# Second product by seven quarter products, with new load order, in a fused attention and feed-forward kernel

## The chip, the cores and the metric

One core of a Trainium2 chip. The metric is the device time of one execution in microseconds (us). Several executions of each kernel were timed, alternating with the kernel before on the same chip; the median is quoted. All runs in this document were in the normal (fast) state. TensorE's granted clock varies within an execution.

## The reference, cut to what matters

```python
# q, k, v: 8 batches x 8 heads x 576 positions x 64;  w_in: 512x2048;  w_out: 2048x512
k_p = k.reshape(B, H, 72, 8, D).mean(axis=3)          # keys and values pooled by 8
v_p = v.reshape(B, H, 72, 8, D).mean(axis=3)
attn = softmax(q @ k_p^T / sqrt(D))
x = (attn @ v_p) -> 4608 tokens x 512
h = x @ w_in;  g = h * sigmoid(h);  out = g @ w_out   # float32, 4608 x 512
```

## The kernel before

The 4608 tokens are worked off in nine tiles of 512. Each tile has a first product ("up", 64 matmuls of 512 columns, and a Silu on ScalarE) and a second product ("down", 64 matmuls of 512 columns). Tile *t* also carries the attention of batch *t* + 1: small pieces are put between the matmuls at numbered steps ("fillers"). The order written here is the order in which each engine's work stands in its timeline. A "tree" below is the pooling of one batch's k or v on VectorE.

```python
def load_one(b, name, eng=None):          # all of k or v of a batch: 72 x 4096 fp32
    ...
    raw = raw_tile(name, SP, POOL)
    (eng or nc.sync).dma_start(out=raw, in_=src)

def tree(dst, raw):                       # pooling by 8: three adds on VectorE
    w = POOL * D // 2
    while w > D:
        nc.vector.tensor_add(out=raw[:, :, :w], in0=raw[:, :, :w], in1=raw[:, :, w : 2 * w])
        w //= 2
    nc.vector.tensor_add(out=dst, in0=raw[:, :, :D], in1=raw[:, :, D : 2 * D])
...
def down(t, h_T, fillers, ms, last=False):
    ...
            for g in range(KG):                      # 16 blocks of the hidden size
                for m, ps in zip(mm, o_ps):          # token blocks of 128
                    ...
                    nc.tensor.matmul(ps[:, cs], lhsT=h_T[g][:, m * 128 : (m + 1) * 128],
                                     rhs=w_out_sb[:, g, cs], start=(g == 0), stop=(g == KG - 1))
            ... copy to o_sb on VectorE, four stores per token block on SyncE ...
...
for t in range(NT):
    a = t + 1                                        # the batch whose attention runs beside
    ...
    f_up.append((at["k"], lambda: pool_k(a)))        # step 0 of the first product (t > 0)
    f_to.append((50 if t else 13, lambda: pool_v(a)))
    f_to.append((0, lambda: load_q(a + 1)))          # GpSimd's queue
    f_to.append((1, lambda: load_one(a + 1, "k", eng)))              # SyncE's queue
    f_to.append((51 if t else 14, lambda: load_one(a + 1, "v", eng)))
```

The softmax here doesn't subtract the row's maximum and nothing guards it: scores larger than these inputs give would overflow.

## Time and profile before

| | |
|---|---|
| median | 325.02 us (324.83 to 325.92) |
| profiled span, mean granted clock | 323.8 us, 0.989 |
| first tile with all of the start | 0 to 65.73 us |
| second to seventh tile | 33.08 us each |
| eighth tile (no attention beside) | 27.62 us |
| last tile with the tail | 31.97 us |

Three more rows of the busy time by stretches, for the first, the eighth and the last tile, are compared with the changed kernel later (columns: stretch, length, then busy us and count of TensorE, weight loads, VectorE, ScalarE, GpSimd; then granted clock, DMA share, GB/s):

```profile
0.00:65.73 65.73, 57.09 (x477) 34.21 (x478) 32.19 (x53) 33.20 (x70) 15.83 (x28) 0.95 0.98 229
264.21:291.83 27.62, 27.62 (x129) 12.51 (x128) 2.77 (x4) 11.21 (x18) 0.00 (x0) 1.00 0.16 41
291.83:323.80 31.97, 27.83 (x145) 13.90 (x142) 3.62 (x6) 9.92 (x17) 0.00 (x0) 1.00 0.16 42
```

In the eighth tile TensorE's busy time is the whole length; in the last, 4 us of the length are not TensorE's.

### The profile page before, as it was taken

The numbers are of one execution on the slowest core, as the hardware profiler recorded it, in microseconds if no ns is written. First come the engines' busy times: TensorE is split into PE (matmuls) and PEld (weight loads), VectorE is DVE, ScalarE is ACT, GpSimd is POOL, SyncE is SP. The second block draws the span as 40 slices with busy tenths as digits, with TensorE's granted clock in tenths as the row PEclk, the third lists the DMA queues.
The fourth block names the chain that finished last, engine by engine and source line by source line (L and its number), as shares of the span: only waits on it lengthen the run. The fifth ranks groups of instructions, "written<-read, shape, count | busy, mean of one in ns | idle before, by whom it ended". The sixth has DMA issues, their size and how long they took to land.

```text
span 323.8 us, 5075 instructions
## 1 busy us (share of the span) xinstructions
PE 311.0 (96%) x2032; PEld 157.0 (48%) x2032; DVE 141.6 (44%) x219; ACT 176.5 (55%) x308; POOL 18.7 (6%) x32
## 2 busy tenths in 40 slices
PE   7899958999999999999999999999999999999994
PEld 3767533444444544454445444544454444444443
DVE  5444761386237633763375337542755230010011
ACT  1478723466656665666565656565656567405500
POOL 5930000000000000000000000000000000000000
PEclk9999995999999999999999999999999999999999
DMA  7999998728722772278327832635200220031023
GB/s 275 257 210 258 238 209 199 200 70 179 180 61 64 171 187 68 66 161 183 88 68 151 178 102 65 145 87 129 65 0 2 65 60 8 7 86 39 0 51 83
DMA packets 23280, 38.15 MB, mean 118 GB/s; under 512 B 3032, under 2 KB 7384, under 8 KB 23256
## 3 DMA queue, kind: packets, MB, share of 16 engines
q1 hardware_dynamic: 16008, 27.73, 32.8%
q0 software_dynamic: 6192, 8.32, 15.4%
q10 hardware_dynamic: 1056, 1.77, 1.5%
q8 instruction: 16, 0.26, 0.4%
q14 instruction: 8, 0.07, 0.1%
HBM read 36.70 MB, written 9.44 MB: 142 GB/s over the span
## 4 chain that ended last, share of the span: by engine, by line
PE 82%; DMA 15%; POOL 1%; issue 1%; SPq 0%; DVE 0%; ACTq 0%; ACT 0%; POOLq 0%
PE o_ps L317 37%; PE hp_ps L286 34%; DMA w_out_sb<-in_moe_w_out_dram 10%; PE sc_ps L199 4%; DMA w_in_sb<-in_moe_w_in_dram 3%; PE nu_ps L243 2%; PE den_ps L221 2%; DMA q_st<-in_q_dram 2%; PE qT_ps L128 2%; POOL w_in_sb L385 1%; SPq L301 0%; DMA out_dram<-o_sb 0%; ACTq L358 0%; PE kT_ps L173 0%; POOL w_out_sb L396 0%
## 5 line engine op out<-in xcount | busy, mean ns | idle before, releaser
L317 PE MATMUL o_ps<-w_out_sb,h_T 128*128 128x512 bf16 (+1 forms) x592 | 143.6, 378 | 4.4 <-DMA w_out_sb<-in_moe_w_out_dram 3.9
L286 PE MATMUL hp_ps<-xT,w_in_sb 128*128 128x512 bf16 (+2 forms) x620 | 131.1, 364 | 0.6 <-ACT h_T L292 0.6
L292 ACT ACTIVATE h_T<-hp_ps 128x512 bf16<-128x512 f32 (+2 forms) x155 | 87.6, 567 | 58.4 <-PE hp_ps L286 57.6
L286 PEld LDWEIGHTS <-w_in_sb 128*128 128x128 bf16 x620 | 59.0, 98 | 57.7 <-issue 1.3
L317 PEld LDWEIGHTS <-h_T 128*128 128x128 bf16 x592 | 55.9, 99 | 60.7 <-issue 11.5
L212 ACT ACTIVATE es<-sc_ps 72x576 bf16<-72x576 f32 x57 | 36.9, 647 | 47.4 <-PE sc_ps L199 47.3
L329 DVE COPY o_sb<-o_ps 128x512 f32<-128x512 f32 (+1 forms) x36 | 24.5, 682 | 83.0 <-PE o_ps L317 82.2
L153 DVE TENSOR_TENSOR raw<-raw 72x2048 f32<-72x2048 f32 (+1 forms) x28 | 49.0, 1750 | 5.0 <-DMA raw<-in_k_dram 4.5
L251 DVE TENSOR_TENSOR xT<-nu_ps,rec 128x288 bf16<-128x288 f32 x64 | 26.2, 453 | 52.1 <-ACT rec L231 33.8
L199 PE MATMUL sc_ps<-qT,kz 128*72 128x288 bf16 x114 | 24.0, 294 | 0.8 <-DVE qT L134 0.7
L134 DVE COPY qT<-qT_ps 128x640 bf16<-128x640 bf16 (+1 forms) x32 | 14.6, 458 | 20.2 <-PE qT_ps L128 20.0
L199 PEld LDWEIGHTS <-kz 128*72 128x72 bf16 x128 | 14.6, 116 | 15.2 <-issue 3.2
L230 ACT ACTIVATE lnd<-den_ps 128x288 f32<-128x288 f32 x30 | 12.1, 402 | 10.1 <-PE den_ps L221 10.1
L128 PEld LDWEIGHTS <-q_bf 128*128 128x128 bf16 x144 | 10.5, 98 | 8.6 <-issue 2.0
L260 ACT ACT_TABLE_LOAD x8 | 10.3, 1283 | 6.7 <-DMA k_st<-in_k_dram 6.6
L243 PE MATMUL nu_ps<-es,vp 72*32 72x288 bf16 x256 | 13.5, 287 | 0.4 <-DVE xT L251 0.4
L231 ACT ACTIVATE rec<-lnd 128x288 f32<-128x288 f32 x30 | 13.3, 442 | 0.9
L117 POOL DMA_DIRECT2D q_bf<-in_q_dram x7 | 5.0, 713 | 151.1 <-PE qT_ps L128 150.3
L128 PE MATMUL qT_ps<-ident,q_bf 128*128 128x128 bf16 x144 | 13.1, 219 | 0.6 <-ACT kz L431 0.6
L263 ACT ACT_TABLE_LOAD x9 | 11.5, 1283 | 0.2
L180 DVE COPY kz<-kT_ps 64x288 bf16<-64x288 bf16 x28 | 8.5, 305 | 4.7 <-PE kT_ps L173 4.3
L221 PE MATMUL den_ps<-es,ones 72*32 72x288 bf16 x128 | 10.2, 296 | 0.0
(41 smaller groups left out, 82.8 us busy)
## 6 DMA issues: line engine op xcount, KB each, us to landing
out_dram<-o_sb SPq DMA_DIRECT2D x140, 64.0 KB
raw<-in_k_dram SPq DMA_DIRECT2D x7, 1152.0 KB
raw<-in_v_dram SPq DMA_DIRECT2D x7, 1152.0 KB
q_bf<-in_q_dram POOLq DMA_DIRECT2D x7, 576.0 KB, 6.1
w_in_sb<-in_moe_w_in_dram POOLq DMA_DIRECT2D x8, 256.0 KB, 8.4
w_out_sb<-in_moe_w_out_dram POOLq DMA_DIRECT2D x4, 512.0 KB, 26.1
q_st<-in_q_dram SPq DMA_DIRECT2D x2, 320.0 KB
v_st<-in_v_dram SPq DMA_DIRECT2D x2, 288.0 KB
```

The costliest lines, as they stand in the source:

```text
L128: nc.tensor.transpose(qT_ps[:, j, :], st["q_bf"][:, a, 2 * D * (j0 + j) : 2 * D * (j0 + j + 1)], ident,)
L134: (copy or nc.vector.tensor_copy)(dst[:, a, j0 : j0 + n], qT_ps.rearrange("d j (s p) -> d j s p", p=QP))
L153: nc.vector.tensor_add(out=raw[:, :, :w], in0=raw[:, :, :w], in1=raw[:, :, w : 2 * w])
L199: nc.tensor.matmul(sc[u][:, :HS], lhsT=kz[b % 2][:, f, 2 * pr + u, :], rhs=st["qT"][:, 2 * pr + u, :], start=True, stop=True,)
L212: nc.scalar.activation(es, sc_ps[:, :, :HS], func=AF.Exp, scale=score_scale)
L221: nc.tensor.matmul(den_ps[32 * hh : 32 * (hh + 1), :HS], lhsT=ones, rhs=es[hh // 2][:, hh % 2, :], start=True, stop=True,)
L243: nc.tensor.matmul(nu_ps[32 * hh : 32 * (hh + 1), :HS], lhsT=st["vp"][:, 4 * g + hh, c::2], rhs=es[hh // 2][:, hh % 2, :], start=True, sto ...
L251: nc.vector.tensor_mul(out=xT[:, 2 * g + c, cols], in0=nu[c][:, :HS], in1=rec)
L286: nc.tensor.matmul(hp_ps[:, :n], lhsT=w_in_sb[:, kk, g * 128 : (g + 1) * 128], rhs=xT[:, kk, t * NTT + n0 : t * NTT + n0 + n], start=(kk = ...
L292: nc.scalar.activation(h_T[g][:, n0 : n0 + n], hp_ps[:, :n], func=AF.Silu)
L317: nc.tensor.matmul(ps[:, cs], lhsT=h_T[g][:, m * 128 : (m + 1) * 128], rhs=w_out_sb[:, g, cs], start=(g == 0), stop=(g == KG - 1),)
L329: nc.vector.tensor_copy(out=o_sb[:, cs], in_=ps[:, cs])
```

## The change

Its intent is to take an eighth of the second product's work from TensorE. In tiles 1 to 8 the 2 x 2 x 2 quarter products become Strassen's seven, for which sums of halves of the hidden tile (VectorE, every tile) and of the second weight (GpSimd, once) are needed. To make room on VectorE, the first of the three pooling adds is done by the load: SyncE loads the first half of every pooled group and GpSimd's queue adds the other half onto it while loading. Batch 1's loads come in pieces by heads, batch 2's later, behind the first stores, so that they do not share the DMA engines with the second weight. ("Half" and "rest" below are these two parts of one load; "hidden sums" and "weight sums" are the sums that the seven products need.) Batch 0's attention is reordered to give ScalarE its exps back to back. The last tile's stores are split over two queues.

```diff
+    def load_rest(b, name):
+        nc.gpsimd.dma_start(out=batches[b][f"{name}_raw"],
+                            in_=source(b, name)[:, :, PH:], accum_op=ALU.add)
+    def hidden_sum(n, k0, k1):                 # five sums, 128 x 2048 bf16 each, in pieces
+        nc.vector.tensor_tensor(out=h_sum[n][:, ks, :], in0=quarter(*a, ks), in1=quarter(*b, ks), op=op)
+    def weight_sum(n, i):                      # five sums in four pieces of 128 x 512 bf16
+        nc.gpsimd.tensor_tensor(out=out, in0=in0, in1=in1, op=op)
+    def down_quarters(t, fillers, last=False):
+        ...                                    # 7 x 16 matmuls of 256 columns in three banks
 ... in the loop over the tiles:
+        if t == 0:                             # three sums into w_sum, second product of tile 0
+            for i in range(PW):
+                for n in range(2, 5):
+                    f_down.append((30 + 8 * i, lambda n=n, i=i: weight_sum(n, i)))
+        if t == 1:                             # two sums in place, first product of tile 1
+            for n in range(2):
+                for i in range(PW):
+                    f_up.append((12, lambda n=n, i=i: weight_sum(n, i)))
-            f_to.append((50 if t else 13, lambda: pool_v(a)))
+            f_to.append((10 if t else 13, lambda: pool_v(a)))
-                f_to.append((1, lambda: load_one(a + 1, "k", eng)))
-                f_to.append((51 if t else 14, lambda: load_one(a + 1, "v", eng)))
+                f_to.append((1 if t else 34, lambda: load_one(a + 1, "k")))
+                f_to.append((2 if t else 44, lambda: load_rest(a + 1, "k")))
+                f_to.append((11 if t else 36, lambda: load_one(a + 1, "v")))
+                f_to.append((12 if t else 54, lambda: load_rest(a + 1, "v")))
 ... cut: the new places of scores and values, batch 0's order, batch 1's loads by heads, the last stores
```

## The prediction

> **What bounds the kernel now.** I read the page's busy table first, then the chain of waits, then the busy time by stretches, and last the timeline of the stretches in which the chain is not TensorE.
>
> ```profile
> PE 311.0 (96%) x2032; PEld 157.0 (48%) x2032; DVE 141.6 (44%) x219; ACT 176.5 (55%) x308; POOL 18.7 (6%) x32
> ...
> PE 82%; DMA 15%; POOL 1%; issue 1%; SPq 0%; DVE 0%; ACTq 0%; ACT 0%; POOLq 0%
> ```
>
> The second line is the chain that ended last: 82% of the span is TensorE, 15% is DMA, and no vector or scalar engine counts. The chain in order of time shows where each part lies (start, length, what):
>
> ```profile
> 11.12 8.14 DMA w_in_sb<-in_moe_w_in_dram
> 20.75 31.10 DMA w_out_sb<-in_moe_w_out_dram
> ...
> 264.21 13.81 PE hp_ps L286 x64
> 278.02 13.81 PE o_ps L317 x64
> 291.83 13.81 PE hp_ps L286 x64
> 305.65 10.37 PE o_ps L317 x48
> 318.82 1.41 DMA out_dram<-o_sb
> ```
>
> So there is a DMA-bound start up to 51.9 us, and after it a TensorE stream with no gap. In it 64 matmuls of 512 columns take 13.81 us, 215.8 ns each. The busy time by stretches says the same for the tiles that carry an attention batch beside (six equal ones, 65.7 to 264.2; columns: length, then busy and count of TensorE, weight loads, VectorE, ScalarE, GpSimd):
>
> ```profile
> 65.73:98.81 33.08, 33.08 (x216) 16.06 (x214) 17.17 (x26) 20.35 (x35) 0.72 (x1) 1.00 0.53 122
> 98.81:131.89 33.08, 33.08 (x216) 16.06 (x214) 17.17 (x26) 20.37 (x35) 0.72 (x1) 1.00 0.53 122
> ```
>
> TensorE is busy in all of the 33.08 us; VectorE has 16 us free, ScalarE 13. Of the 33.08, 27.62 are the two products and 5.46 attention.
>
> In the first tile TensorE waits for the second weight three times (last bracket: idle time before, and what ended it), for 3.9 us in sum, and is slowed by its clock as well (the page's clock row falls to 5 tenths for one slice of 8.1 us):
>
> ```profile
> 42.29 0.38 PE L317 MATMUL o_ps<-w_out_sb,h_T 128*128 128x512 bf16 x1 [0.84 <-DMA w_out_sb<-in_moe_w_out_dram]
> ...
> 47.60 0.81 PE L317 MATMUL o_ps<-w_out_sb,h_T 128*128 128x512 bf16 x3 [2.16 <-DMA w_out_sb<-in_moe_w_out_dram]
> ...
> 51.89 1.44 PE L317 MATMUL o_ps<-w_out_sb,h_T 128*128 128x512 bf16 x3 [0.88 <-DMA w_out_sb<-in_moe_w_out_dram]
> ```
>
> SyncE's queue shows what runs beside that weight: the loads of batch 2, not needed before 66 us.
>
> ```profile
> 37.96 0.30 SPq L147 DMA_DIRECT2D raw<-in_k_dram  x1
> 48.94 0.30 SPq L147 DMA_DIRECT2D raw<-in_v_dram  x1
> ```
>
> **What the Trainium skill says.** "TensorE: Matmul & The Clock Gate", section "Back-to-back issue gap", gives N/2.4 + 2.5 ns for a warm matmul of N columns: 215.8 ns at 512 and 109.2 at 256. The trace agrees at 512, and nearly at 256. The last token block is multiplied in two halves of 16 matmuls of 256 columns, and VectorE's copies before and after the first half start 1.74 us apart, 108.8 ns per matmul:
>
> ```profile
> 316.05 0.69 DVE L329 COPY o_sb<-o_ps 128x512 f32<-128x512 f32 x1 [2.76 <-PE o_ps L317]
> 317.79 0.42 DVE L329 COPY o_sb<-o_ps 128x256 f32<-128x256 f32 x1 [1.05 <-PE o_ps L317]
> ```
>
> Each of these needs its own weight load (98 to 99 ns in the groups), and that just hides in 108.8. "VectorE: DVE Perf Modes", "The perf-mode tier table", gives a two-input op of 2048 elements 2293 ns in fp32 and 1224 in bf16 in SBUF. The trace has the first (72x2048 f32: 2278 ns) and no op of the second kind. "GPSIMD Engine Reference", "4.1 Engine selection", calls GpSimd about 2 times slower than VectorE for two-input work; no such op is in this trace. "DMA: Bandwidth & Descriptors", "Issuing engines are not separate DMA queues", says that transfers of all issuers interleave on the same 16 engines; the chunks of the second weight, coming 5.3 and 4.3 us apart beside SyncE's loads, agree.
>
> **The change, part by part.**
>
> *Seven products, tiles 1 to 8.* 64 matmuls of 512 columns become 7 x 16 = 112 of 256 columns: 112 x 108.8 ns = 12.19 us for 13.81, a gain of 1.62 us per tile. For the seven tiles 1 to 7 that is 11.3 us.
>
> *What it adds on VectorE* per tile, beside TensorE: five sums of halves of the hidden tile, 10,240 bf16 elements in eleven instructions, an estimate of 6.5 us at the skill's bf16 rate (about 12 if it ran at the fp32 rate); and seven evacuations of about 0.69 us for four (+2.1). What it takes away: the first 2048-element add of k's and of v's tree, now done by an accumulating load (2 x 2.28 = 4.6 us). VectorE goes from 17.2 to some 21 us of 31.5, off the path. The order on the engine matters more. The sums that need the last hidden tile come after its Silu (0.6 us, about 0.85 after the last matmul), but the first 24 matmuls (2.6 us) of the seven products need only earlier parts, so nothing waits. Small returns I do see: the second matmul group of the next tile takes the bank whose last add ends about 0.9 us after the tile while 0.86 us of cover stand before it; and scores now come 7 or 8 matmuls of 0.109 us apart with one score buffer, where matmul to free buffer takes 0.44 + 0.65 us (a score's start to its exp, and the exp, in the timeline). Both are near ties. I give 0.25 us back per tile, 1.8 in seven.
>
> *Last tile.* Before, its second product runs from 305.65 to 320.2 (14.5 us: 0.52 us of wait for a bank between the halves), then 3.6 us of copies one behind the other and a store. After: 12.2, plus 0.4 for ScalarE, which issues half of 32 small stores at some 0.43 us and copies besides, and a tail shorter by 0.4. Gain 2.3 us.
>
> *First tile.* The two halves of batch 1's k and v move the same bytes as before. Batch 2's loads now stand on SyncE behind the stores of the first two token blocks, so they no longer share engines with the second weight. Up to 42 us nothing is relieved (batch 1's loads run until then). After it, chunks that came every 5.3 and 4.3 us should come every 3.1 (an estimate: 1 KB packets of this queue take 97 ns in the trace, 32 of them per engine and chunk), at 45.3 and 48.4 instead of 47.6 and 51.9. The rest of the tile took 13.7 us from there, some 1.8 of it at half clock. I expect the clock to drop again, since TensorE will wait even earlier (the reordered batch 0 frees it about 1.5 us sooner, into the same DMA wait). The next tile should start near 61.5 instead of 65.7: 4.2 us gained. The back-to-back exps gain nothing of their own.
>
> *Second tile.* Here I expect a new wait. SyncE issues batch 2's halves only after eight stores of the first tile, near 56 us. GpSimd then waits for the half of k, issues the accumulating rest, does six weight sums (estimate 1.2 us each: 512 elements at twice VectorE's time) and only then issues v's rest, near 67; it lands near 71. VectorE's order has v's tree in the first fifth of the second tile, ahead of the copies that free the transposes' banks. TensorE can go on to about the 36th matmul (near 69.5) and then waits: 1 to 6 us, and I take 3.5.
>
> Sum: 325.0 - 11.3 + 1.8 - 2.3 - 4.2 + 3.5 = 312.5 us.
>
> **The rivals.**
> 1. *Weight loads become the bound.* Each 109 ns matmul needs a 98 ns load, and any break (a score with another shape, a semaphore) shows. For it: after attention groups the profile has weight loads with 0.24 to 0.33 us of "issue" idle. Against it: TensorE does not idle there now, and the 16 matmuls above ran at 108.8. At 120 ns per matmul the tiles give back 1.25 us each: 321.
> 2. *VectorE becomes the bound* because the bf16 sums run at the fp32 rate. Then it has about 27 of 31.5 us, and the sums just before the second product come 1 to 1.5 us late: +8 to 11 us, 320 to 323. Operands are 16-bit, in SBUF, in runs of 256, so I hold it unlikely.
> 3. *The second tile's wait does not come* because GpSimd is quicker than I think or the halves land sooner: 309. *Or it is worse*, if accumulating loads are slow and GpSimd starves beside VectorE: 317.
> 4. *The start is bound elsewhere.* If the weight's chunks come no sooner, 4 us are lost: 316.5; if the clock stays full, 2 are won: 310.5.
>
> **Range and chances.** The term for the products is sure in size (two measured spacings). The two large unknowns, first and second tile, are each plus or minus 3 us and partly of opposite sign; the steady give-back may be 0 to 0.6 us a tile (plus or minus 2). Together 306.5 to 318. Faster by over 2% means below 318.5: chance 0.89. Within 2%: 0.09, rival 2 or two bad cases together. Slower: 0.02.
>
> **What would show it.** Right: tiles 2 to 6 of 31.5 to 31.8 us with TensorE busy throughout; the tile without attention at 26.0 to 26.3; sums of 1024 bf16 elements near 0.65 us; the second weight's last wait ended near 48; a TensorE gap of a few us near 68 to 75, released by VectorE copies that wait for batch 2's v. Wrong: a spacing of the 256-column matmuls above 112 ns in the tile without attention (rival 1); sums of 1.2 us (rival 2); no gap in the second tile (rival 3); a last wait for the second weight still at 51 (rival 4). What would overturn all: transposes or scores waiting for late keys in every tile, if the accumulating loads took over 25 us each.

## The result, and the profile after

The changed kernel takes 333.55 us (median of 4, 333.13 to 334.43), the one before 324.92 in the same rounds: 1.0271 of it, 95% interval 1.023 to 1.0312. It is slower by 2.7%. Ratios here are the mean time of one kernel's fast runs over that of the other's fast runs of the same rounds, so not quite the ratio of the medians quoted.

The page of the changed kernel: busy times, then TensorE and its clock in 40 slices of 8.3 us.

```profile
PE 303.3 (92%) x2394; PEld 192.6 (58%) x2394; DVE 194.2 (59%) x326; ACT 178.2 (54%) x310; POOL 60.4 (18%) x64
...
PE   7899999906929999999999999999999999999994
...
PEclk9999999966769999999999999999999999999998
```

TensorE is busy for 7.7 us less than before (311.0 to 303.3), and is still idle for longer: slices 9 to 12 (0, 6, 9, 2) stand for a hole between 66 and 100 us, and the clock drops there. The busy time by stretches puts it into one tile, the second:

```profile
0.00:60.15 60.15, 54.77 (x471) 32.17 (x472) 38.96 (x60) 33.03 (x69) 24.21 (x33) 1.00 0.89 204
60.15:115.52 55.37, 37.86 (x264) 22.69 (x262) 29.22 (x38) 20.85 (x35) 22.71 (x20) 0.82 0.60 110
115.52:147.18 31.66, 31.66 (x263) 20.72 (x262) 20.77 (x38) 20.49 (x34) 3.55 (x3) 1.00 0.66 127
...
273.83:299.87 26.04, 26.04 (x178) 17.20 (x176) 11.20 (x18) 10.84 (x17) 0.00 (x0) 1.00 0.18 43
299.87:331.30 31.43, 26.36 (x177) 17.01 (x174) 10.98 (x20) 11.04 (x20) 0.00 (x0) 0.96 0.28 66
```

Tile by tile, against before: first 65.73 to 60.15 (-5.6), second 33.08 to 55.37 (+22.3), third to seventh 33.08 to 31.66 (five times -1.42, -7.1), eighth 27.62 to 26.04 (-1.6), last 31.97 to 31.43 (-0.5). The sum is +7.5 us, the difference of the profiled spans (323.8 to 331.3). So everything but the second tile gained, and the second tile alone lost more than all gains.

TensorE's timeline of that tile has three long waits (last bracket: idle time before, and what ended it):

```profile
74.16 0.42 PE L215 MATMUL kT_ps<-ident,kp 72*128 72x72 bf16 x4 [8.11 <-DVE kp L191]
...
82.50 0.44 PE L141 MATMUL qT_ps<-ident,q_bf 128*128 128x128 bf16 x5 [2.81 <-DVE qT L147]
...
97.27 0.61 PE L428 MATMUL o_psP<-w_out_sb,h_sum 128*128 128x256 bf16 x2 [6.59 <-DVE h_sum L383]
```

They make 17.5 us. Against the later tiles (31.66) the second lost 23.7; the other 6.2 are TensorE's busy time, 37.86 for the same matmuls, at a mean clock of 0.82 in this stretch (0.51 from 74.2 to 79.7 us, 0.57 from 82.5 to 86.4, 0.67 from 97.3 to 101.5: each behind one of the waits). All three waits end with VectorE. VectorE's own timeline says what it waited for:

```profile
72.16 1.22 DVE L187 TENSOR_TENSOR raw<-raw 72x1024 f32<-72x1024 f32 x1 [11.27 <-DMA raw<-in_k_dram]
...
79.50 1.22 DVE L187 TENSOR_TENSOR raw<-raw 72x1024 f32<-72x1024 f32 x1 [5.41 <-DMA raw<-in_v_dram]
...
87.89 12.47 DVE L383 TENSOR_TENSOR h_sum<-h_T 128x1024 bf16<-128x1024 bf16 x8 [0.85 <-ACT h_T L330]
```

The first two rows are late loads: k's rest landed at 72.2, v's at 79.5. The third is of another kind. Eight sums of the hidden tile took 12.47 us with no wait in between (in the undisturbed run below they need 3.9, in two groups of 2.57 and 1.36), and the list of that line's durations has a longest of 9322 ns with a median of 679. GpSimd's timeline shows what it did meanwhile:

```profile
63.55 1.46 POOL L168 DMA_DIRECT2D raw<-in_k_dram  x1 [10.07 <-PE hp_ps L324]
64.49 7.20 POOL L406 TENSOR_TENSOR w_sum<-w_out_sb 128x512 bf16<-128x512 bf16 x6
71.13 1.94 POOL L168 DMA_DIRECT2D raw<-in_v_dram  x1
...
87.22 9.43 POOL L406 TENSOR_TENSOR w_out_sb<-w_out_sb 128x512 bf16<-128x512 bf16 x8
```

From 64.5 to 71 six weight sums stood between k's rest and v's rest. From 87.2 to 96.7 GpSimd did the eight weight sums in place, and VectorE's long sum started at 87.9 and ended at 97.2. The chain that ended last passes v's rest with 8.35 us from issue to landing, and that one sum with 9.33 us:

```profile
71.13 8.35 DMA raw<-in_v_dram
...
87.89 9.33 DVE h_sum L383
```

### The profile page after: what moved, and what is told of

Its sections match the earlier page's. It is cut to its first block, busy times and chain, and to the rows that moved or that the text cites. A ratio compares the mean times of both kernels' runs of the same rounds, so it can differ in the third digit from the quotient of the medians.

```text
span 331.3 us, 5963 instructions
## 1 busy us (share of the span) xinstructions
PE 303.3 (92%) x2394; PEld 192.6 (58%) x2394; DVE 194.2 (59%) x326; ACT 178.2 (54%) x310; POOL 60.4 (18%) x64
## 4 chain that ended last, share of the span: by engine, by line
PE 79%; DVE 7%; issue 4%; POOL 4%; DMA 4%; ACT 0%; POOLq 0%; DVEq 0%
PE hp_ps L324 35%; PE o_psP L428 13%; PE o_psQ L428 13%; PE o_psR L428 4%; PE sc_ps L241 4%; POOL w_sum L406 3%; DVE h_sum L383 3%; DMA raw<-in_v_dram 3%; PE qT_ps L141 2%; PE nu_ps L285 2%; PE den_ps L263 2%; PE v_ps L578 2%; DMA k_st<-in_k_dram 1%; DVE raw L187 1%; PE sc_mm L241 1%
## 5 line engine op out<-in xcount | busy, mean ns | idle before, releaser
L383 DVE TENSOR_TENSOR h_sum<-h_T 128x1024 bf16<-128x1024 bf16 (+2 forms) x88 | 60.7, 736 | 31.4 <-ACT h_T L330 31.4
L428 PEld LDWEIGHTS <-h_sum 128*128 128x128 bf16 x640 | 62.1, 99 | 19.4 <-DVE h_sum L383 7.1
L254 ACT ACTIVATE es<-sc_ps 72x576 bf16<-72x576 f32 x56 | 36.2, 647 | 34.8 <-PE sc_ps L241 34.0
L293 DVE TENSOR_TENSOR xT<-nu_ps,rec 128x288 bf16<-128x288 f32 x64 | 26.3, 452 | 31.3 <-ACT rec L273 30.1
L187 DVE TENSOR_TENSOR raw<-raw 72x1024 f32<-72x1024 f32 (+1 forms) x20 | 24.8, 1240 | 20.7 <-DMA raw<-in_k_dram 15.1
L428 PEld LDWEIGHTS <-h_T 128*128 128x128 bf16 x256 | 24.0, 98 | 6.3 <-issue 3.4
L428 PE MATMUL o_psP<-w_out_sb,h_sum 128*128 128x256 bf16 x128 | 18.8, 285 | 6.6 <-DVE h_sum L383 6.6
L406 POOL TENSOR_TENSOR w_sum<-w_out_sb 128x512 bf16<-128x512 bf16 x12 | 16.2, 1602 | 20.3 <-DMA w_out_sb<-in_moe_w_out_dram 20.3
L428 PE MATMUL o_psQ<-w_out_sb,h_T 128*128 128x256 bf16 x128 | 18.4, 273 | 0.3 <-DVE rr_sb L443 0.3
L428 PE MATMUL o_psP<-w_out_sb,h_T 128*128 128x256 bf16 x128 | 18.4, 273 | 0.0
L428 PE MATMUL o_psR<-w_sum,h_sum 128*128 128x256 bf16 x128 | 18.4, 273 | 0.0
L351 PE MATMUL o_ps<-w_out_sb,h_T 128*128 128x512 bf16 x64 | 17.1, 379 | 0.3
## 6 DMA issues: line engine op xcount, KB each, us to landing
q_bf<-in_q_dram POOLq DMA_DIRECT2D x7, 576.0 KB, 12.7
raw<-in_v_dram POOLq DMA_DIRECT2D x6, 576.0 KB, 10.4
```

Source lines behind the costliest of these rows:

```text
L254: nc.scalar.activation(es, sc_ps[:, :, :HS], func=AF.Exp, scale=score_scale)
L293: nc.vector.tensor_mul(out=xT[:, 2 * g + c, cols], in0=nu[c][:, :HS], in1=rec)
L351: nc.tensor.matmul(ps, lhsT=h_T[:, g, m * 128 : (m + 1) * 128], rhs=w_out_sb[:, g, :], start=(g == 0), stop=(g == KG - 1),)
L383: nc.vector.tensor_tensor(out=h_sum[n][:, ks, :], in0=quarter(*a, ks), in1=quarter(*b, ks), op=op)
L406: nc.gpsimd.tensor_tensor(out=out, in0=in0, in1=in1, op=op)
L428: nc.tensor.matmul(ps[b][:, c, :], lhsT=left(n, kt, c), rhs=W_OUT[n][:, kt, :], start=b not in begun, stop=kt == KQ - 1, skip_group_check= ...
```

## The experiments

Two theories. **Late loads:** batch 2's halves stand behind stores, their rests behind GpSimd's weight sums, and the rests are slow to land. **Contention:** a two-input sum on GpSimd holds up VectorE's two-input sums. Here the Trainium skill has a sentence that I had not used: "SBUF — State Buffer", section "Who interferes with whom", says that a VectorE instruction with two inputs in the on-chip buffer contends with a GpSimd instruction that reads it, and not with one that only writes it. Rivals: the data dependence (the seven products wait for the weight sums' results), and the seven products themselves.

The twelve kernels ran on three chips, four, four and four; only runs of one chip are compared by their medians, others by their ratio to the kernel before (1% is 3.25 us). "Second tile" below is the time from its first matmul to that of the third tile, in the profiled run; before it is 33.08 us, in the changed kernel 55.37.

### Undo one of the two, or both

**Weight sums on VectorE** (the late loads stay):

```diff
-        nc.gpsimd.tensor_tensor(out=out, in0=in0, in1=in1, op=op)
+        nc.vector.tensor_tensor(out=out, in0=in0, in1=in1, op=op)
```

> The changed kernel with its 20 weight sums on VectorE instead of GpSimd, nothing else. Theory L (late loads: batch 2's halves are issued behind eight stores of the first tile, and the accumulating rests come after that): the wait of 8.1 us for the pooled keys in the second tile stays at 7 to 8.5 us, v's rest comes some 6 us earlier, the second tile goes from 55.4 to 42 to 47 us, the whole to 322 to 326 us. Theory C (contention: the sums on GpSimd slow VectorE and hold up GpSimd's queue, and this is the loss): the second tile falls under 38 us and the whole under 317 us.

Measured: 323.46 us (322.91 to 323.89), 0.9973 of the kernel before (0.9938 to 1.0009). The second tile is 45.5 us; TensorE's wait for the hidden sums is gone, those for k (5.70 us) and for the copies of the queries' transposes (3.85) remain. So about 10 us of the 23.7 go with GpSimd's sums. The tile and the whole are what the late-load theory gave; its 7 to 8.5 us for k is not, since that wait fell as well. The traces point to a reason: the first stores and batch 2's halves behind them were issued 3.0 us earlier than in the changed kernel (the halves at 53.73 us against 56.76). There, six of GpSimd's sums (44.48 to 53.48) fall on VectorE's pooling of v in the first tile and lengthen it, and VectorE's copies for the first stores come behind that pooling. The same adds in the changed kernel and here:

```profile
43.46 2.77 DVE L187 TENSOR_TENSOR raw<-raw 72x1024 f32<-72x1024 f32 x2
...
43.51 1.93 DVE L187 TENSOR_TENSOR raw<-raw 72x1024 f32<-72x1024 f32 x2
```

**Batch 2's loads early, whole, by heads** (the sums stay on GpSimd): the four loads go to SyncE at steps 14 and 15 of the first tile's second product, ahead of its stores, with no accumulating rest.

```diff
+                    f_to.append((14, lambda: load_heads(2, "k", ("v_raw", "k_st"))))
+                    f_to.append((15, lambda: load_heads(2, "v", ("k_raw", "q_st"))))
```

> The changed kernel with batch 2's k and v loaded in full by heads (as batch 1's are), issued when batch 1's v is pooled and ahead of the stores, no accumulating load for this batch; weight sums stay on GpSimd. Theory L: no wait for pooled keys, no half clock, second tile 34 to 40 us, whole 312 to 318 us. Theory C: the wait for the hidden sums before the second product (6.6 us) stays or grows, as the in-place weight sums still run beside VectorE; second tile 42 us or more, whole above 320 us.

Measured: 322.2 us (321.85 to 322.78), ratio 0.9937 (0.9902 to 0.9972). The second tile is 45.8; the wait for k is gone, one for a copy of a transpose is 2.46, and that for the hidden sums is 6.62, as in the changed kernel, and one VectorE sum again took 9.3 us beside GpSimd's eight. These are the contention theory's numbers (42 us or more, above 320). So each theory won one of the two runs, and neither is the whole.

**Both:**

```diff
+        nc.vector.tensor_tensor(out=out, in0=in0, in1=in1, op=op)
+                    f_to.append((14, lambda: load_heads(2, "k", ("v_raw", "k_st"))))
+                    f_to.append((15, lambda: load_heads(2, "v", ("k_raw", "q_st"))))
```

> Both edits together. If the two causes are all there is, the second tile takes 32 to 36 us (31.7 as the later ones, plus VectorE's extra 5.5 us of trees and 3 us of weight sums, of which some may show) and the whole 309 to 314 us. If the seven products or their sums themselves hurt there (theory S), it stays above 40 us and 318.

Measured: 316.51 us (315.88 to 317.92), ratio 0.9762 (0.9711 to 0.9813). The second tile is 39.7: both of the expected ranges are missed, it lies between them. One wait is left (5.09 us for a copy of a transpose): VectorE now had the longer trees (9.3 us, three adds for each load again) and the in-place weight sums (2.76 us) ahead of those copies. That this order makes the wait is a reading so far; later runs take the causes away.

**The new loads with the plain second product** (no seven products, no sums, the old places of scores and values):

```diff
-        if t == 0:
-            down(t, f_down, [(0, 1), (2,), (3,)])
-        else:
-            down_quarters(t, f_down, last=t == NT - 1)
+        ms = [(0, 1), (2,), (3,)] if t == 0 else [(m,) for m in range(NTT // 128)]
+        down(t, f_down, ms)
```

> The changed kernel with the plain second product in all tiles: no weight sums, no hidden sums, only the new loads and the new order of batch 0. Theory L: the first tile ends near 60 us as in the changed kernel, the second tile waits 8 us or so for the pooled keys and runs part of its time at half clock (45 to 48 us instead of 33.1), so that the whole is 328 to 334 us: the loads alone are slower than before. Theory S or C: no wait of over 2 us in the second tile, whole 318 to 322 us.

Measured: 327.87 us (326.81 to 328.86), ratio 1.011 (1.0068 to 1.0151). The second tile is 42.1 with waits of 5.39 and 1.47 us although no weight sum and no hidden sum competes: the late loads alone cost some 9 us (somewhat less than the 45 to 48 us expected). The later tiles take 33.07, as before the change. So the seven products are worth 1.41 us a tile (33.07 to 31.66), and the new loads neither help nor hurt there.

### Both causes taken away with the change's own loads

**Halves and rests early, sums on VectorE:** batch 2's halves and accumulating rests are issued at steps 14 and 15 of the first tile's second product into buffers that are free by then, and the in-place weight sums go to the second tile's second product.

```diff
-                    f_up.append((12, lambda n=n, i=i: weight_sum(n, i)))
+                    f_down.append((4 + 8 * i, lambda n=n, i=i: weight_sum(n, i)))
+                kt, vt = ("k_raw", "v_raw") if t else ("v_raw", "k_raw")
-                f_to.append((1 if t else 34, lambda: load_one(a + 1, "k")))
+                f_to.append((1 if t else 14, lambda: load_one(a + 1, "k", kt)))
 ... k's rest 44 -> 15, v's half 36 -> 14, v's rest 54 -> 15; weight sums on nc.vector
```

> The changed kernel with weight sums on VectorE (the eight in-place ones spread over the second tile's second product), and batch 2's halves and accumulating rests kept but issued as soon as batch 1's v is pooled, ahead of the stores. If late loads and the overlap of GpSimd's sums with VectorE's were the whole loss, and the 8 us left in the run with both edits were VectorE's longer trees and early weight sums, the second tile takes 31.7 to 33.5 us and the whole 307 to 311 us. If something else in the second tile costs time, it stays above 36 us and the whole above 313.

Measured: 312.42 us (311.51 to 314.19, 6 runs), ratio 0.9618 (0.9589 to 0.9647). The second tile is 34.8, with one wait of 2.78 us. Both numbers are a little above the expected ones (31.7 to 33.5, 307 to 311) and below those of "something else" (36, 313); the last wait is taken up at the end.

**The same loads, the sums back on GpSimd** at the change's places:

```diff
-        nc.vector.tensor_tensor(out=out, in0=in0, in1=in1, op=op)
+        nc.gpsimd.tensor_tensor(out=out, in0=in0, in1=in1, op=op)
-                    f_down.append((4 + 8 * i, lambda n=n, i=i: weight_sum(n, i)))
+                    f_up.append((12, lambda n=n, i=i: weight_sum(n, i)))
```

> As e5 with the weight sums back on GpSimd at the places of the change. Contention: although the loads are in time, the hidden sums before the second product of the second tile are held up for most of the 13 us of GpSimd's in-place sums, the wait of about 6.6 us is back, second tile 42 to 47 us, whole 319 to 324 us. If only the late loads mattered: within 2 us of e5.

Measured: 328.51 us (328.07 to 329.04), ratio 1.0103 (1.0071 to 1.0135). The second tile is 52.6. That is more than the 42 to 47 us (319 to 324) expected: not only the hidden sums were held, but k's pooling too. (The 13 us in the expectation is a slip; GpSimd's in-place sums took 9.43 us in the changed kernel.) With no late load left, TensorE waits 8.06 us for k and 7.48 for the hidden sums. VectorE and GpSimd in this run:

```profile
62.83 9.22 DVE L187 TENSOR_TENSOR raw<-raw 72x1024 f32<-72x1024 f32 x1 [3.22 <-DMA raw<-in_k_dram]
...
81.26 13.35 DVE L383 TENSOR_TENSOR h_sum<-h_T 128x1024 bf16<-128x1024 bf16 x8 [0.85 <-ACT h_T L330]
```

```profile
57.12 13.84 POOL L406 TENSOR_TENSOR w_sum<-w_out_sb 128x512 bf16<-128x512 bf16 x12
...
81.48 9.43 POOL L406 TENSOR_TENSOR w_out_sb<-w_out_sb 128x512 bf16<-128x512 bf16 x8
```

An add of 1.22 us took 9.22, and it ended at 72.05 where GpSimd's twelve sums had ended at 70.96. Contention alone thus costs 17.8 us of the tile (52.6 against 34.8), late loads alone 10.7 (45.5 against 34.8), both 20.6; in the first two, the place of the in-place sums is a second difference. They do not add up, and the traces name two reasons: while k's rest is late, the second run of weight sums meets no pooling add; and in the changed kernel part of the lateness itself comes from GpSimd's sums in the first tile (see "Weight sums on VectorE").

### What in GpSimd's sums does it

The next three experiments leave the early-halves kernel as it is, with its real weight sums on VectorE, and add 20 idle GpSimd instructions of 128x512 bf16 at the change's places, whose results nobody reads.

**Idle two-input sums** (the change's own, into a spare tile):

```diff
+        nc.gpsimd.tensor_tensor(out=warm.rearrange("p (k c) -> p k c", c=CQ), in0=in0, in1=in1, op=op)
+                    f_down.append((30 + 8 * i, lambda n=n, i=i: idle_sum(n, i)))   # tile 0
+                    f_up.append((12, lambda n=n, i=i: idle_sum(n, i)))             # tile 1
```

> As the run with idle copies, but the 20 idle GpSimd instructions are the change's own two-input sums, written into a tile that nobody reads. If my theory holds, that the instructions themselves block VectorE and not the wait for their results: as in the run with GpSimd's real sums and early loads, one VectorE sum of 9 us or so, twice; second tile 48 to 54 us, median 324 to 330. If the cause was the data dependence (the seven products waiting for GpSimd's late results): second tile under 37 us, median under 314.

Measured: 323.21 us (322.84 to 324.12), ratio 0.9927 (0.9884 to 0.9971), against 0.9618 without them: some 10 us more; second tile 45.8. Nobody waits for these results, so a loss of 11.0 us in the tile comes without the data dependence (the real sums on GpSimd lost 17.8). But my numbers were missed by a little (48 to 54 us, 324 to 330), and in an instructive way: no VectorE sum was held for 9 us; the longest took 2.5. Many were lengthened instead.

```profile
63.37 1.89 DVE L187 TENSOR_TENSOR raw<-raw 72x1024 f32<-72x1024 f32 x1
65.29 1.52 DVE L191 TENSOR_TENSOR kp<-raw 72x512 bf16<-72x512 f32 x1
```

```profile
57.34 18.77 POOL L412 TENSOR_TENSOR warm<-w_out_sb 128x512 bf16<-128x512 bf16 x12
```

Compare the durations of single GpSimd sums, first in the run with GpSimd's real sums, then here (lists by line: shortest, median, longest in ns):

```profile
L406 POOL TENSOR_TENSOR w_sum<-w_out_sb x12: 1630/1670/1719, 57.1 to 69.3; 128x512 bf16<-128x512 bf16 x12
```

```profile
L412 POOL TENSOR_TENSOR warm<-w_out_sb x20: 1152/1216/2084, 57.3 to 88.9; 128x512 bf16<-128x512 bf16 x20
```

In the real run twelve sums of 1.67 us would be 20.0 us one after the other, but they took 13.84: they overlap, each being recorded as begun some 0.56 us before the one ahead has ended (the profile calls its GpSimd spans rough). In the idle run they do not overlap: the first twelve took 18.77 us with hardly a gap (17.73 us busy in the 18.60 from 57.4 to 76.0), because GpSimd's sums were lengthened there as VectorE's were (1.15 us the shortest, 2.08 the longest). That all of them write the same tile may be what keeps them apart; no run tests it. Real sums show both forms too: the first run of them in the changed kernel (from 44.48 us) and in the run with early loads by heads does not overlap, and there the longest of VectorE's adds took 2.17. So in these traces an overlapping run of GpSimd sums held VectorE's sum to the end of the run (four runs met one, for 9.2 to 10.2 us), and a run without overlap lengthened VectorE's sums one at a time. In the traces of the changed kernel, of the run with early loads by heads and of the run with GpSimd's real sums, the five overlapping runs were all right behind a load issued by GpSimd; the two runs that came behind a wait did not overlap. But the idle sums stood behind such a load as well and did not overlap. What starts the overlap no run settles.

**Idle one-input copies:**

```diff
-        nc.gpsimd.tensor_tensor(out=warm.rearrange("p (k c) -> p k c", c=CQ), in0=in0, in1=in1, op=op)
+        nc.gpsimd.tensor_copy(out=warm.rearrange("p (k c) -> p k c", c=CQ), in_=in0)
```

> The early-halves kernel (312.4 us, real weight sums on VectorE) with 20 idle GpSimd instructions put where the change has its weight sums: one-input copies of 128x512 bf16 out of the second weight into a tile that nobody reads. Nothing waits for their results. If GpSimd's reading of the on-chip buffer alone holds up VectorE's two-input sums[...]: a single VectorE sum of 2 us or more beside them, second tile over 37 us, median 315 or more. If it takes two inputs on GpSimd, or if the real sums' results were what was waited for: no VectorE sum over 1.5 us there, median 311.5 to 313.5.

Measured: 318.62 us (316.89 to 319.12), ratio 0.9765 (0.971 to 0.982), second tile 41.3. The time is on the side of "reading alone is enough", 1.5% of the kernel before, some 4.8 us, over the kernel without them (by the ratios), and 6.5 in the second tile; the detail I gave for it was wrong, since the longest VectorE sum took 1.42 us in place of 1.22, and eight hidden sums 6.95 us in place of 3.9. Reading one input is enough to slow VectorE:

```profile
77.44 6.95 DVE L383 TENSOR_TENSOR h_sum<-h_T 128x1024 bf16<-128x1024 bf16 x8 [0.85 <-ACT h_T L330]
```

**Idle memsets** (GpSimd only writes):

```diff
+        nc.gpsimd.memset(warm, 0.0)
```

> As the run with idle copies, but the 20 idle GpSimd instructions only write (memsets of 128x512 bf16). If the contention is over reading, no VectorE sum is held: none over 1.5 us, second tile 34.5 to 35.3 us, median 311.5 to 313.5. If GpSimd's writing, or its mere running, holds VectorE: sums of 2 us or more and a median of 315 or more.

Measured: 312.66 us (311.56 to 316.17), ratio 0.9618 (0.9547 to 0.9688); the kernel without them has the same ratio. The longest VectorE sum is 1.22 us, and the eight hidden sums take 3.93:

```profile
76.39 2.57 DVE L383 TENSOR_TENSOR h_sum<-h_T 128x1024 bf16<-128x1024 bf16 x5 [0.85 <-ACT h_T L330]
79.84 1.36 DVE L383 TENSOR_TENSOR h_sum<-h_T 128x512 bf16<-128x512 bf16 x3 [0.89 <-ACT h_T L330]
```

The second tile was 35.7, somewhat above my 34.5 to 35.3: TensorE was busy for 33.5 us of it at a clock of 0.95, and waited 2.17 for a transpose's copy. GpSimd was not idle: the memsets ran for 12.7 us in all, the copies for 17.5. So it is GpSimd's reading, not its running or writing, that VectorE meets. This is what the skill's sentence says.

### The tail, the start, and the last wait

**Sixteen whole-row last stores instead of 32 half rows**, on the early-halves kernel:

```diff
-            if last:
-                store(t, 2 + cc[0], LO, both)
-                store(t, c, LO if last else FULL, both if last else (nc.sync,))
+                store(t, c, FULL, both if last else (nc.sync,))
 ... likewise for the other half
```

> As e5, and in the last tile one store of whole rows where there were two of half rows: 16 stores of 64 KB over both queues instead of 32 of 32 KB. If the issue of small stores makes the tail (SyncE issues 16 in 9.1 us in the changed kernel, ending 2 us after the last sum), the tail from the last matmul to the end falls from 4.9 to 3.2 to 3.8 us and the whole by 1 to 1.7 us against e5. If the tail is landing time alone, within 0.4 us of e5.

Measured: 312.86 us (310.39 to 313.97), ratio 0.9613 (0.9578 to 0.9648), the same as with 32 stores (0.9618). The 1 to 1.7 us that fewer stores might have gained did not come; the result is the expectation's other case, give or take: the number of stores does not bound the tail. In both, the last issues end near 307.4 us and the span some 3.1 us later.

**Batch 0 in its old order**, on that last kernel:

```diff
-    scores(0, 0, 0, fill=2, split=True)
-    scores(0, 1, 0, fill=2, split=True)
-    scores(0, 0, 1, fill=2, split=True)
+    for pr in range(2):
+        scores(0, pr, 0, fill=2, split=True)
-    denominators(0, 0, 0, on_dve=True)
-    pool_members(0, 0, 4)
+    pool_members(0, 0, VI)
 ... and so on, the order of the kernel before
```

> As e6 with batch 0's scores, denominators and value pooling in the order of the kernel before. If the new order gains nothing (in the changed kernel the first matmul of the first product starts at 22.1 us, before at 21.9), within 0.7 us of e6. If it gains, 1 to 2 us slower than e6.

Measured: 314.28 us (312.11 to 315.76), ratio 0.9664 (0.9619 to 0.971), against 0.9613 with the new order. The median is 1.4 us longer, which is the case of "it gains" in the expectation, but the intervals overlap: two of the four runs took some 312.5 us, two 315.7, at a slightly lower clock. The first tile's first product begins at 21.88 us with the old order and at 22.12 in the changed kernel. Whether the reordering gains anything, these runs cannot tell from their spread.

**v's tree later**, on the early-halves kernel, to see whether the last 2.8 us come only from VectorE's order:

```diff
-            f_to.append((10 if t else 13, lambda: pool_v(a)))
+            f_to.append((45 if t == 1 else 10 if t else 13, lambda: pool_v(a)))
 ... v's half and rest of batch 3 behind it (46, 47); k always in the one buffer, v in the other
```

> The early-halves kernel (312.4 us) with one thing moved: in the second tile VectorE does v's tree after the copies of the queries' transposes (step 45 instead of 10 of the first product), and batch 3's half and rest of v move behind it. My theory: the 2.8 us that TensorE still waited there came only from v's rest landing ahead of those copies in VectorE's order; second tile 31.9 to 32.5 us instead of 34.8, median 309 to 310.5. Rival: the wait passes to another place of the same tile (batch 2's vp, or batch 3's halves in the third tile), second tile or third tile longer by 2 us or more and the median stays at 312.

Measured: 309.04 us (308.3 to 309.35), ratio 0.9485 (0.9444 to 0.9525). It beats both kernels: 5.2% under the one before. Its second and third tile:

```profile
59.75:91.42 31.67, 31.67 (x264) 20.73 (x263) 23.16 (x46) 20.48 (x34) 3.55 (x3) 1.00 0.85 156
91.42:123.07 31.65, 31.65 (x264) 20.69 (x262) 20.77 (x38) 20.47 (x34) 3.55 (x3) 1.00 0.67 128
```

TensorE is busy for all of both, at full clock. The second tile's loss of 23.7 us is gone to the last tenth, with the seven products, the accumulating loads and the five weight sums all still there.

| kernel | weight sums | batch 2's loads | second tile, us | ratio to before |
|---|---|---|---|---|
| before | none | early, whole | 33.1 | 1 |
| changed | GpSimd | late halves | 55.4 | 1.027 |
| sums moved | VectorE | late halves | 45.5 | 0.997 |
| loads moved | GpSimd | early, by heads | 45.8 | 0.994 |
| both moved | VectorE | early, by heads | 39.7 | 0.976 |
| halves early, sums on GpSimd | GpSimd | early halves | 52.6 | 1.010 |
| halves early | VectorE | early halves | 34.8 | 0.962 |
| and v's tree later | VectorE | early halves | 31.7 | 0.949 |

With 2% as the mark and the intervals given, the changed kernel is slower than the one before and the last two rows are faster; 0.976 (and the run with idle copies) is unclear, and the other rows do not differ from it.

## Why the prediction was right or wrong

The prediction was 312.5 us with 318.0 as its upper end, and 0.02 as the chance of a slower kernel; it was 333.55. The step that failed is the **second tile**: "+3.5" for one wait of 1 to 6 us, where the profile shows +23.7. Its parts:

- *The landing.* I had v's rest issued near 67 and landing near 71. It was issued at 71.1, behind the six weight sums, and landed at 79.5: 8.35 us for an accumulating load for which I had allowed 4. For k's rest I foresaw no wait at all, and it cost the first 8.11 us: TensorE stopped after 26 matmuls, near 66 us, for k, and not after about 36, near 69.5, for v. Rival 3 named slow accumulating loads, and gave 4.5 us to it.
- *Contention.* I priced GpSimd's sums at 1.2 us each, and they took that (9.43 us for eight), but by luck: "twice VectorE's time" put VectorE at 0.6 us, where it takes 0.35, and the factor is 3.4. And I asked only how long GpSimd would need. In rival 3 I named only the other direction, GpSimd starving beside VectorE. That exists (GpSimd sums of up to 2.1 us for 1.15 in the runs without overlap), but in the second tile the runs show VectorE's sums held by GpSimd's reads, up to 9.3 us for a sum of 0.68. In the changed kernel this is the third wait, 6.59 us; with the loads early it is both long waits.
- *The clock.* Behind the waits TensorE's granted clock was as low as 0.51, and the same matmuls took 37.86 us instead of 31.66. I had counted with that in the first tile and not in the second. It is 6.2 us, a quarter of the loss. Not every wait brings it: in the early-halves run the tile with the 2.78 us wait shows a clock of 1.00.

The other terms:

- *Seven products:* right. 31.66 us per tile stands inside the 31.5 to 31.8, and 26.04 in the tile without attention inside 26.0 to 26.3. The gain per tile is 1.42 against the 1.62 - 0.25 = 1.37 of the prediction. Rivals 1 and 2 fall: TensorE is busy throughout, and sums of 1024 bf16 elements take 0.68 us. One reading of the Trainium skill was short: "TensorE: Matmul & The Clock Gate", section "Back-to-back issue gap", calls the formula that of a single matmul by itself, and gives about 131 ns for 512 columns in a stream. This case's stream took the formula's 215.8 ns, so the measurement decides, and the prediction's spacing stands on the trace.
- *First tile:* the direction and most of the size were right, 5.6 us for 4.2, but not the way: no matmul waited for the second weight (its last chunk had landed by 46.9 us, where I had 48.4), and the clock stayed full there, as rival 4's last clause allowed. In the old first tile the half-clock stretch after 52 us is some 3.6 us long and costs 1.8; the prediction gives the cost as the length.
- *Last tile:* over-sized, 0.5 for 2.3. The seven products do run there (12.9 us for 12.2 expected), but the tail behind the last matmul became longer, 4.7 us in place of 3.6. Half as many stores do not shorten it; what sets it stays open.
- *Batch 0's order:* I credited no time of its own to it, and no run shows any beyond its spread. That it would free TensorE about 1.5 us sooner did not happen (22.12 us against 21.90).

With the second tile mended, the other terms add up: 323.8 - 5.6 (first) - 8.5 (six tiles of 1.42) - 1.6 (eighth) - 0.5 (last) = 307.6, and the last experiment's profiled span, on another chip, is 307.4.

## What to carry to other kernels

Before work is given to an idle engine, ask what it shares with the busy one: GpSimd's 20 small sums were only 23 us of an idle engine's time (13.84 + 9.43), and cost the kernel some 16 us (328.51 against 312.42), mainly by holding VectorE, while on VectorE itself they took 0.35 us each. Price a one-off transition (here the tile in which weights are first summed and loads change their form) by the order of each queue and with measured landing times, not as a remainder: it can cost more than six steady tiles gain. And when a change loses, look first at where, tile by tile; here everything but one tile was as predicted, and the mended version is 5.2% faster than the kernel before.

## What the Trainium skill lacked or had wrong

- "SBUF — State Buffer", "Who interferes with whom": right on who meets whom (by the ratios, GpSimd's reads cost some 5 to 16 us, writes only nothing). What it lacks is the size for two-input sums: its sentence that one engine holds the ports for a whole instruction and the other blocks is about VectorE's two-port modes. The runs show a VectorE add of 1.22 us that took 9.22, through about seven GpSimd sums (1.1 us from start to start) that the profile shows overlapping, and 1.89 beside sums that did not overlap.
- "GPSIMD Engine Reference", "4.1 Engine selection": about 2 times slower for two-input work. For 512 bf16 elements per partition it was 3.4 times: 9.43 us for eight on GpSimd, 2.76 on VectorE. One-input work at "roughly line-rate" costs VectorE time too (the kernel lost some 4.8 us to 20 idle copies), which that row does not say; the page on the on-chip buffer does.
- "DMA: Bandwidth & Descriptors" names accumulating loads but I found no duration for one: 576 KB took a median of 8.2 us (k) and 10.4 us (v) from issue to landing in the changed kernel.
